# Nystrom attention and two FFN blocks on one core: scores of two batches as 64x32 products, and a written-out order for the rest of the first FFN block

## The chip, the core and the metric

The kernel runs on one NeuronCore of a Trainium2 chip. The metric is the device time of one execution in microseconds (us), lower is better. Five engines work side by side, each through its own instructions in order: TensorE (PE in the profile), VectorE (DVE), ScalarE (ACT), GpSimd (POOL) and SyncE (SP), which issues the DMA transfers here.

## The reference, cut to what matters

```python
def _attn_ref(q, k, v):                  # 4 batches, 8 heads, 576 tokens, 64 dims
    q_lm = q.reshape(B, H, 32, 18, D).mean(axis=3)     # 32 landmarks of 18 tokens
    k_lm = k.reshape(B, H, 32, 18, D).mean(axis=3)
    A, Bm, C = sm(q, k_lm), sm(q_lm, k_lm), sm(q_lm, k)  # softmax(scale * a @ b.T)
    Z = Bm.T / (norm1(Bm) * norminf(Bm) + 1e-06)
    for _ in range(6):
        Z = 2 * Z - Z @ Bm @ Z
    return A @ Z @ C @ v
x = attn_out as (2304 tokens, 512)
h = x @ w_in;   x = (h * clip(h + 3, 0, 6) / 6) @ w_out            # FFN 1, d_ff 2048
h = x @ w_in2;  out = where(h > 0, h, exp(min(h, 0)) - 1) @ w_out2  # FFN 2, d_ff 2048
```

The four weight matrices arrive as float64 and are converted on the chip.

## The kernel before

**Slots of the first FFN block.** FFN 1 is worked through in 128 slots: 4 batches x 2 halves of 288 tokens x 16 blocks of 128 hidden features. (Batch 0 is cut in 320 and 256 tokens.) A slot `i` has two parts. `slot_a1(i)` makes one `h` tile in PSUM by six matmuls (two head groups x three products of high and low parts, `h<-at..,n..`), then ACT takes the Relu (`gf<-h`), DVE multiplies (`gf<-gf,h`), ACT casts the high part (`gh<-gf`) and POOL subtracts for the low part (`gl`). `slot_a2(i - 3)` multiplies the result of three slots ago with `w_out`: four output tiles x three products, twelve matmuls `x<-g..,wo`. The pool for `h` has two PSUM banks, that for `x` four.

**Attention beside the slots.** While the slots of one batch run, the attention of the next is computed in two PSUM banks (`bk`, pool `pa`). Heads come in two groups `g` of four. Per group, `prep` sums tokens to landmarks (`lm`) and POOL lays them out block-diagonally (`bd`, half zeros). `score_b`, `score_c` and `soft` make the three score matrices from `bd` as 128x64 products, two matmuls `pr` beside each other for a half of 288 tokens. `values` transposes the exponentials (`ident,EC`) and multiplies with V (`vt,ect`). `inverse` is the iteration for Z (`BD`, `BT`, `X`), `finish` joins the two (`X,t`). `attn_n` multiplies the outcome (`mt`) with FFN 1's first weights, eight matmuls of 64x32 by 512 columns (`w1c,mt`), and splits them into the `nh`, `nl` that the slots use; `attn_at` does it for A.

**Conversion.** `conv_out2` and `conv_in2` turn 32 pieces of FFN 2's weights from float64 to float32: a load `u` of 512 KB, two ACT steps, two DVE steps, one POOL step (`y`), a store.

**Order.** Up to slot 35 the order of every engine is that of the code (`strict[0]` true: `InOrder` chains each engine's instructions), and the strings `PLAN` and `PLAN1` say in which order the generators take their steps; a letter is one step. From slot 36 (`END`) on `strict[0]` is false: each step is recorded with a due time (`wanted`), and a scheduler orders the engines. `newton(b)` sets the due times of a batch's attention by the slot; `attn_n` and `attn_at` are called at fixed slots (`NAT` = 25, 28, 31 and the batch's first slot); one conversion starts every second slot (`O2`); the loads of FFN 2's input (`load_x(0)`) go one step per slot from slot 100. FFN 2 then runs as 24 `quartet`s of seven products.

Of the kernel before, what the change touches and what calls it, by code (L numbers as in the profile page):

```python
# [10 lines left out]
F32 = mybir.dt.float32  # L11
# [20 lines left out]
def nystrom_ffn_kernel(ctx: ExitStack, tc, q, k, v, w_in1, w_out1, w_in2, w_out2, out):  # L32
# [325 lines left out]
    def conv_out2(kk):  # L358
        to_dram(wo2d[kk], part(w_out2, kk, 0))

    def conv_in2(m, kk):

        to_dram(wi2d[m, kk], w_in2[m, kk], 4)

# [85 lines left out]
    def load_in2(q):  # L450
# [3 lines left out]
        for kk in range(2):  # L454
# [25 lines left out]
            sub(f[:, 0], l[:, 0], f[:, 0])  # L480
            act.copy(out=hr[:, 0:3], in_=l[:, 0:3])
            sub(lr[:, 0:3], l[:, 0:3], h[:, 0:3], pool)
            act.copy(out=hr[:, 3:7], in_=f)
# [7 lines left out]
    kt_t, qt_t, kbd_t, qbd_t, kl_t = {}, {}, {}, {}, {}  # L491

    def load_qk(b, g, what):
        t = ap_.tile([128, 2, S], F32, name=what + "t", tag=what + "t", bufs=2)
        gated(sp.dma_start(out=t, in_=(k if what == "k" else q)[b, g]))
        raw_t[b, g, what] = t
# [128 lines left out]

    def values(b, g, EC, cvs, sc):
# [5 lines left out]
        for j in range(RUN):  # L632
            atr(ct[j // JB][0:PRUN, 128 * (j % JB):128 * (j % JB) + 128], EC[:, j:S:RUN], ident)
        yield 1.0
# [111 lines left out]

    def newton(b):

        EB, sb, sc, cvs = newton_tiles()
        s = [SB * (b - 1) + (NEW if b > 1 else NEW1)]  # L750
        kept = {}

        def go(gen, n=99):
            for _ in range(n):
                wanted(s[0])
                try:
                    s[0] += next(gen) * (PACE if b > 1 else PACE1)
                except StopIteration:
                    return

        def keep(key, gen):
            kept[key] = yield from gen

        go(prep(b, 0))
        go(score_b(b, 0, sb, EB))
        go(keep(0, score_c(b, 0, sc)))
        go(soft(b, 0))
        go(values(b, 0, kept[0], cvs, sc))
        go(prep(b, 1))
        go(score_b(b, 1, sb, EB))  # L770
        inv = keep("Q", inverse(EB, sb))
        sC = keep(1, score_c(b, 1, sc))
        sA = soft(b, 1)
        go(inv, 1)
        go(sC, 2)
        go(inv, 1)
        go(sC)
        go(inv, 2)
        go(sA, 3)
        go(inv, 2)  # L780
        v1 = values(b, 1, kept[1], cvs, sc)
        go(v1, 2)
        go(inv, 2)
        go(sA)
        go(v1)
        go(inv)
        go(finish(b, kept, cvs, sc))

# [498 lines left out]
    def first_half(units, n0):  # L1287
# [38 lines left out]
        for i in range(NKT, END):  # L1326
# [12 lines left out]
    def second_half(slots):  # L1339
# [30 lines left out]
        for e in (act, vec, pool):  # L1370
            e.flow = e.last

# [33 lines left out]
    banks["att"] = ctx.enter_context(tc.tile_pool(name="pa", bufs=2, space=PSUM))  # L1406
    second_half(first_half(units, n0))
    strict[0] = False

    newton(2)  # L1410
    conv = [lambda kk=kk: conv_out2(kk) for kk in range(NKT)]
    conv += [lambda m=m, kk=kk: conv_in2(m, kk) for m in range(NQ) for kk in range(2)]
    for i in range(END, NA):
        b, r = i // SB, i % SB

        wanted(i)
        if r == 0:
            run(attn_n(b, NW - 1))
            run(attn_at(b, 1))
            if b + 1 < B:  # L1420
                newton(b + 1)
# [113 lines left out]
```

## Time and profile before

| | us |
|---|---|
| median of 3 runs | 814.88 (811.93 to 817.96) |
| the profiled execution | 813.47 |
| its span, first to last instruction | 811.7 |

| engine | busy us | share of the span |
|---|---|---|
| PE matmul | 784.1 | 97% |
| PE weight load | 696.9 | 86% |
| DVE | 540.6 | 67% |
| ACT | 461.9 | 57% |
| POOL | 417.3 | 51% |

Durations of matmuls overlap in the profile, since the engine is pipelined: where matmuls follow each other without a wait, the distance from start to start is what one costs. The share of busy time is a mean over stages that have different limits.

### The profile page before, as it was taken

To read this page: it belongs to the slowest core of one execution; us is meant where nothing else is said; L and a number is where in the kernel's file an instruction comes from. 1 tells how busy PE (TensorE), PEld (TensorE's weight loads), DVE (VectorE), ACT (ScalarE), POOL (GpSimd) and SP (SyncE) were. 2 spreads that over 40 slices of the span, in tenths; PEclk is the share of its full clock that TensorE was granted. 3 is DMA by queue.
4 is the path that set the end of the run, shared out by engine and by line. 5 is a ranking of instruction groups with operands and counts; after the bars stand their busy time and mean duration, and the time that the engine had idled before them with its cause. 6 is when DMAs were issued, how large, how long until landed. Compare 5 with 4: busy or idle time off the path is not lost.

```text
span 811.7 us, 16375 instructions
## 1 busy us (share of the span) xinstructions
PE 784.1 (97%) x5928; PEld 696.9 (86%) x5928; DVE 540.6 (67%) x1092; ACT 461.9 (57%) x1012; POOL 417.3 (51%) x423
## 2 busy tenths in 40 slices
PE   7799999999999999989999999999999999999998
PEld 6566678789887889879999998888898989999998
DVE  6899577478645764477345777766655655777795
ACT  3687454666556556584545566556544644555562
POOL 2576476467554565456420786769652550223311
PEclk9899999999999999999999999999999999999999
DMA  9977932786577445752241777689999666877653
GB/s 323 405 221 234 284 118 90 204 267 217 193 231 251 149 144 177 230 192 105 91 173 60 256 262 272 223 309 344 387 381 316 215 223 249 273 237 256 228 183 124
DMA packets 115601, 184.58 MB, mean 227 GB/s; under 512 B 8576, under 2 KB 71552, under 8 KB 115520
## 3 DMA queue, kind: packets, MB, share of 16 engines
q1 hardware_dynamic: 115520, 183.54, 66.5%
q8 instruction: 47, 0.77, 0.4%
q14 instruction: 34, 0.28, 0.1%
HBM read 130.02 MB, written 53.48 MB: 226 GB/s over the span
## 4 chain that ended last, share of the span: by engine, by line
PE 64%; DMA 11%; DVE 9%; ACT 5%; issue 3%; POOL 3%; SPq 1%; DVEq 0%; ACTq 0%; POOLq 0%
PE x L116 33%; PE h L116 27%; PE bk L116 4%; DMA u<-in_moe_w_in 4%; DMA u<-in_moe_w_out 2%; DMA qt<-in_q 2%; DMA w<-wo2d 1%; DVE h L116 1%; DVE u L116 1%; DVE gf L116 1%; ACT gf L116 1%; SPq L116 1%; DVE lm L116 1%; DVE y L116 1%; DMA x<-wo2d 1%
## 5 line engine op out<-in xcount | busy, mean ns | idle before, releaser
L116 PE MATMUL h<-x,wi 128*128 128x384 f32 x1008 | 204.8, 338 | 2.2 <-ACT a L116 1.3
L116 PE MATMUL x<-gh,wo 128*128 128x288 f32 (+1 forms) x896 | 199.3, 297 | 1.0 <-ACT xs L116 0.5
L116 PEld LDWEIGHTS h<-x,wi 128*128 128x128 f32 x1008 | 177.7, 188 | 13.5 <-DVE u L116 2.5
L116 PEld LDWEIGHTS x<-gh,wo 128*128 128x128 f32 x896 | 149.6, 188 | 9.2 <-issue 6.0
L116 PE MATMUL x<-gl,wo 128*128 128x288 f32 (+1 forms) x448 | 130.7, 294 | 0.0
L116 POOL TENSOR_TENSOR gl<-gf,gh 128x288 fp32r<-128x288 f32 (+1 forms) x100 | 85.0, 853 | 76.9 <-ACT gh L116 70.5
L116 ACT CAST gh<-gf 128x288 fp32r<-128x288 f32 (+2 forms) x160 | 72.5, 454 | 88.1 <-DVE gf L116 87.8
L116 PE MATMUL x<-w,gh 128*128 128x512 f32 (+1 forms) x360 | 101.8, 356 | 0.1
L116 PE MATMUL h<-atl,nh 128*128 128x288 f32 (+2 forms) x256 | 82.3, 321 | 7.8 <-DVE gf L116 3.0
L116 DVE SCALAR_TENSOR_TENSOR gf<-gf,y 128x384 f32<-128x384 f32 x80 | 65.6, 820 | 35.6 <-ACT gf L116 35.5
L116 DVE SCALAR_TENSOR_TENSOR gf<-gf,h 128x288 f32<-128x288 f32 (+1 forms) x112 | 49.4, 443 | 55.2 <-ACT gf L116 54.5
L116 PEld LDWEIGHTS x<-gl,wo 128*128 128x128 f32 x448 | 84.3, 188 | 1.1 <-issue 0.9
L116 ACT ACTIVATE gf<-h,half_b 128x288 f32<-128x288 f32 (+2 forms) x128 | 63.5, 499 | 35.9 <-PE h L116 30.9
L116 PE MATMUL x<-w,ghl 128*128 128x512 f32 (+1 forms) x324 | 76.7, 357 | 0.1
L116 PE MATMUL h<-ath,nl 128*128 128x288 f32 (+2 forms) x256 | 76.7, 300 | 0.0
L116 ACT ACTIVATE gf<-y 128x384 f32<-128x384 f32 x80 | 42.0, 525 | 60.4 <-DVE y L116 60.4
L116 PE MATMUL h<-ath,nh 128*128 128x288 f32 (+2 forms) x256 | 76.4, 298 | 0.0
L116 PEld LDWEIGHTS x<-w,gh 128*128 128x128 f32 x360 | 64.7, 189 | 6.4 <-ACT gh L116 0.5
L116 PEld LDWEIGHTS h<-atl,nh 128*128 128x128 f32 x256 | 48.6, 190 | 22.7 <-issue 9.0
L116 PE MATMUL x<-w,gl 128*128 128x512 f32 (+1 forms) x180 | 64.2, 357 | 0.0
L116 POOL TENSOR_TENSOR x<-u,gf 128x384 f32<-128x384 f32 x16 | 18.1, 1156 | 84.8 <-DVE gf L116 50.9
L116 PEld LDWEIGHTS x<-w,ghl 128*128 128x128 f32 x324 | 55.2, 189 | 5.9 <-DVE ghl L116 0.3
(182 smaller groups left out, 1522.6 us busy)
## 6 DMA issues: line engine op xcount, KB each, us to landing
wi<-wi2p SPq DMA_DIRECT2D x64, 448.0 KB, 5.9
wi2p<-wi SPq DMA_DIRECT2D x32, 448.0 KB, 2.8
u<-in_moe_w_in SPq DMA_DIRECT2D x25, 512.0 KB, 5.1
w1c<-w1d SPq DMA_DIRECT2D x48, 256.0 KB, 4.6
w<-wo2p SPq DMA_DIRECT2D x24, 512.0 KB, 6.7
ub<-in_moe_w_out SPq DMA_DIRECT2D x16, 512.0 KB, 10.2
u<-in_moe_w_out SPq DMA_DIRECT2D x16, 512.0 KB, 5.6
wo2p<-w SPq DMA_DIRECT2D x16, 512.0 KB, 3.4
```

What stands on the lines that cost most here:

```text
L116: inst = getattr(self.eng, name)(*a, **kw)
```

## The change

1. For batches 2 and 3 `prep8` sums the landmarks without the division and without `bd`; key landmarks stand in the first 32 columns of the key tile (`n + S` = 608 columns). `products` makes the scores of both groups at once from 64x32 pieces: eight matmuls, four column places x two row halves, each group into a bank of its own. The host lays the heads of odd groups out with row halves swapped, so that the eight pieces lie apart (`a ^ g`).
2. `score_c8` makes the landmark scores and the first half of C in one go (32 + 288 columns); the first half is copied out of PSUM over the keys, so that the second half can have the banks. `soft8` works in the same way by halves.
3. From slot 36 to the end of the first block `strict[0]` stays true. `PLAN2` and `PLAN3` (320 letters each, 160 of them slot steps `s`) write out the order of batches 2 and 3 with the slots (five `s` each) and the conversions (`z`, five each); `ending` does it for slots 100 to 127.
4. `conv_stream` issues each conversion's load one conversion ahead; its `z` steps are used up around slot 90. `load_in2` becomes a generator whose steps are spread from slot 114 on, and `load_x(0)` goes one step per slot from slot 104.

```diff
+    def products(ps, w, x, gs):
+        for pr in range(2):
+            for a in range(2):
+                o = 64 * pr + 32 * a
+                for i, g in reversed(list(enumerate(gs))):
+                    r = slice(64 * (a ^ g), 64 * (a ^ g) + 64)
+                    amm(ps[i][o:o + 32, :], w[i][r, pr, :], x[i][r, pr, :], True, True)
...
+    def score_c8(b, gs, sc, first):
...
+        cut = 0, 32 + HALF, 32 + S
+        ps = []
+        for hf in range(2):
+            ps.append([bank()[:, 0:cut[hf + 1] - cut[hf]] for _ in gs])
+            if hf == 0:
+                first.extend(ps[0])
+            products(ps[hf], ql, [t[:, :, cut[hf]:cut[hf + 1]] for t in kt], gs)
+            yield 0.4
+            if hf == 0 and b:
+                for i in n:
+                    act.copy(out=EC[i][:, 0:HALF], in_=ps[0][i][:, 32:])
...
+        for i, g in enumerate(gs):
+            for hf in (1, 0):
+                act.activation(
+                    out=EC[i][:, hf * HALF:(hf + 1) * HALF], in_=ps[hf][i], func=AF.Exp,
...
+    def soft8(b, gs):
...
+        for hf in range(2):
+            sa.append([bank()[:, 0:HALF] for _ in gs])
+            products(sa[hf], [t[:, :, 0:32] for t in kt], [t[:, :, hf * HALF:(hf + 1) * HALF] for t in qt], gs)
...
+    def conv_stream():
...
+        nxt = begin()
+        while nxt:
+            (gen, o, y), nxt = nxt, begin()
+            flush()
+            yield
+            for _ in gen:
+                yield
+            pending.append((o, y))
+    PLAN2, PLAN3 = "zppspsssppsssspspszspszzzzszssszzcbzz...", "ppszssppzssspzpzsszspsspsszsszszzzcbsz..."
...
-    newton(2)
-    conv = [lambda kk=kk: conv_out2(kk) for kk in range(NKT)]
...
-        if (i - END) % O2 == 0 and conv:
-            gate[0] = marks["slot"]
-            wanted(i + 4)
-            conv.pop(0)()
...
+    zs = conv_stream()
+    for b, plan in ((2, PLAN2), (3, PLAN3)):
+        third(b, plan, slots_of(SB * b - SB + 4, SB * b + 4), zs)
...
+    ending(slots_of(NA - SB + 4, NA), zs, load_x(0, vec), load_in2(0))
```

On TensorE, at the first scores of batch 2 (slot 38 before, slot 39 in the change): `h` and `x` are the slots' matmuls, `bk` the attention banks. Before, the scheduler put the products of one group between two matmuls of a slot; the three other pairs of keys stand apart further down.

```order
L116 MATMUL x<-gh,wo_1311 128x288
L116 MATMUL h<-atl,nh_1950 128x288
L116 MATMUL bk<-lm,bd 64x32 x2
L116 MATMUL bk<-kt,bd 64x288 x2
L116 MATMUL h<-ath,nl_1951 128x288
```

In the change:

```order
L116 MATMUL h<-ath,nl_1951 128x288
L116 MATMUL h<-ath,nh_1950 128x288
L116 MATMUL bk<-kt,lm 32x320 x8
L116 MATMUL x<-gh,wo_1419 128x288
L116 MATMUL x<-gl,wo_1419 128x288
```

Landmark scores and half of C, of both groups, now stand in one piece of eight matmuls behind the six of a slot.

On TensorE, at the start of Z's iteration in batch 2 (slot 47 before, slot 43 in the change); `BD` and `BT` make the norms and the first product. Before, no score product follows within two slots:

```order
L116 MATMUL bk<-BD,onesbd 128x128
L116 MATMUL x<-gh,wo_1873 128x288
L116 MATMUL x<-gl,wo_1873 128x288
L116 MATMUL bk<-BT 32x32 x8
L116 MATMUL x<-gh,wo_1873 128x288
L116 MATMUL h<-atl,nh_1884 128x288
```

In the change:

```order
L116 MATMUL bk<-BD,onesbd 128x128
L116 MATMUL bk<-BT 32x32 x8
L116 MATMUL x<-gh,wo_1652 128x288
L116 MATMUL x<-gl,wo_1652 128x288
L116 MATMUL x<-gh,wo_1652 128x288
L116 MATMUL bk<-qt,kt 32x288 x8
```

Three matmuls of the slot now stand between the products of `BT` and the query scores, which take both attention banks.

On TensorE, in slot 46 of the change: two rounds of the iteration (`X`) and the products with V stand together, where before a round stood alone or behind all 24 products with V.

```order
L116 MATMUL h<-ath,nh_2094 128x288
L116 MATMUL bk<-X 32x64 x8
L116 MATMUL bk<-vt,ect 32x64 x12
L116 MATMUL bk<-X 32x64 x8
L116 MATMUL bk<-vt,ect 32x64 x12
L116 MATMUL x<-gh,wo_1825 128x288
```

In the whole of slots 36 to 127 the attention's matmuls stand in 53 unbroken pieces before and in 34 in the change.

## Rows read from the trace of the kernel before

**Rows 1.** Windows by stage: length, busy us (count) by engine, PE clock, DMA share, GB/s

```profile
161.07:262.03 100.96, 99.49 (x947) 85.61 (x946) 66.15 (x144) 59.69 (x139) 59.75 (x66) 1.00 0.71 232
262.03:357.45 95.42, 93.26 (x898) 82.81 (x896) 55.74 (x126) 58.51 (x134) 54.95 (x58) 1.00 0.57 184
357.45:428.45 71.00, 69.27 (x516) 68.35 (x517) 38.41 (x77) 37.84 (x87) 30.52 (x30) 1.00 0.35 121
```

**Rows 2.** Timeline of PE: start, us, what, xcount; last slot, then the second block

```profile
426.08 0.29 PE L116 MATMUL h<-atl,nh 128*128 128x288 f32 x1
...
428.46 0.34 PE L116 MATMUL h<-x,wi 128*128 128x384 f32 x1
```

**Rows 3.** Waits of PE from 161 us to 428.5 us: total us, times, longest

```profile
PE h L116 <- DVE gf L116: 3.0, 4, 1.3
PE bk L116 <- DVE nl L116: 1.5, 2, 0.8
PE x L116 <- ACT xs L116: 0.5, 1, 0.5
PE bk L116 <- DVE X L116: 0.2, 1, 0.2
```

**Rows 4.** Timeline of PE around one pair of score products

```profile
171.08 0.71 PE L116 MATMUL bk<-kt,bd 128*64 128x288 f32 x4
171.71 0.40 PE L116 MATMUL h<-atl,nh 128*128 128x288 f32 x1
```

**Rows 5.** Timeline of PE around landmark scores alone

```profile
253.82 0.31 PE L116 MATMUL bk<-lm,bd 128*64 128x32 f32 x4
254.06 0.40 PE L116 MATMUL x<-gh,wo 128*128 128x288 f32 x1
```

**Rows 6.** Timeline of PE around eight 64x32 products, 512 columns

```profile
226.25 0.29 PE L116 MATMUL x<-gh,wo 128*128 128x288 f32 x1
226.48 1.09 PE L116 MATMUL bk<-w1c,mt 64*32 64x512 f32 x16
227.50 0.40 PE L116 MATMUL h<-atl,nh 128*128 128x288 f32 x1
227.74 0.29 PE L116 MATMUL h<-ath,nl 128*128 128x288 f32 x1
```

**Rows 7.** Timeline of PE around eight 64x32 products, 256 columns

```profile
162.62 0.66 PE L116 MATMUL bk<-w1c,mt 64*32 64x256 f32 x16
163.21 0.40 PE L116 MATMUL x<-gh,wo 128*128 128x288 f32 x1
```

**Rows 8.** Timeline of PE around one round of the iteration

```profile
207.55 0.43 PE L116 MATMUL bk<-X 32*32 32x64 f32 x16
207.91 0.40 PE L116 MATMUL h<-ath,nh 128*128 128x288 f32 x1
```

**Rows 9.** Waits of PE from 92 us to 161 us (seven rows, five stand)

```profile
PE bk L116 <- POOL bd L116: 1.7, 2, 1.3
...
PE bk L116 <- DVE nl L116: 0.4, 1, 0.4
PE bk L116 <- ACT EC L116: 0.4, 1, 0.4
PE bk L116 <- DVE X L116: 0.3, 1, 0.3
PE bk L116 <- DVE nn L116: 0.2, 1, 0.2
```

**Rows 10.** Timeline of DVE, start of the iteration in batch 1

```profile
126.28 0.28 DVE L116 TENSOR_REDUCE nn<-bk 128x4 f32<-128x128 f32 x1
...
127.27 0.41 DVE L116 SCALAR_TENSOR_TENSOR X<-bk,cc,istack 128x32 f32<-128x32 f32 x2
```

**Rows 11.** Waits of ACT from 161 us to 357 us, the two for conversion loads

```profile
ACT y L116 <- DMA u<-in_moe_w_out: 14.8, 9, 3.4
ACT y L116 <- DMA u<-in_moe_w_in: 12.3, 7, 3.1
```

**Rows 12.** DMA issues from 161 us to 357 us: count, KB, median us to landing

```profile
u<-in_moe_w_in SPq DMA_DIRECT2D x16, 512.0 KB, 4.9
```

More of the change, by code (lines that the diff above doesn't have):

```diff
@@ L356, in split_out1 @@
         wo[kk] = h, l
[L358 to L363, printed above, removed]
     def scratch(n, w):
@@ L631, in values @@
         ct = [bank(), bank()]
-        for j in range(RUN):
+        for j in [*range(JB, RUN), *range(JB)] if b > 1 else range(RUN):
             atr(ct[j // JB][0:PRUN, 128 * (j % JB):128 * (j % JB) + 128], EC[:, j:S:RUN], ident)
+        if 1 < b < B - 1:
+            load_qk(b + 1, g, "k")
         yield 1.0
@@ L745, in newton_tiles @@
         return EB, sb, sc, cvs
[L747 to L787, printed above, removed]
     PLAN = """
@@ L1325, in first_half, with slots_of @@
         run(ns)
-        for i in range(NKT, END):
+        yield from slots_of(NKT, END)
+    def slots_of(n0, n1):
+        for i in range(n0, n1):
             wanted(i)
@@ new lines, in third, with keep, preps, parts @@
+    def third(b, plan, slots, zs):
+        EB, sb, sc, cvs = newton_tiles()
+        kept, first, gs = {}, [], range(G)
+        def keep(key, gen):
+            kept[key] = yield from gen
+        def preps():
+            for g in gs:
+                yield from prep8(b, g)
+        def parts():
+            for c in range(NW):
+                yield from attn_n(b, c)
+        make = {
+            "p": preps, "c": lambda: keep("C", score_c8(b, gs, sc, first)), "b": lambda: score_b8(gs, first, sb, EB),
+            "i": lambda: keep("Q", inverse(EB, sb)), "a": lambda: soft8(b, gs),
+            "v": lambda: values(b, 0, kept["C"][0], cvs, sc), "V": lambda: values(b, 1, kept["C"][1], cvs, sc),
+            "f": lambda: finish(b, kept, cvs, sc), "n": parts, "t": lambda: attn_at(b, 0), "T": lambda: attn_at(b, 1),
+        }
+        gens = {"s": slots, "z": zs}
+        for c in plan:
+            if c not in gens:
+                gens[c] = make[c]()
+            next(gens[c], None)
+        run(slots)
+        for c in "pcbiavVftnT":
+            run(gens[c] if c in gens else make[c]())
@@ L1375, in nystrom_ffn_kernel, with ending @@
+    def ending(slots, zs, xs, ws):
+        for i in range(NA - SB + 4, NA):
+            for n in range(NDM + 1):
+                next(slots, None)
+                if i < NA - SB + XSET + 4:
+                    next(zs, None)
+                elif n == 2:
+                    next(xs, None)
+                if i >= NA - 14 and n == 4:
+                    next(ws, None)
+        run(slots)
+        run(zs)
+        run(xs)
+        run(ws)
     win, xp = [], []
```

149 lines of the change are left out of this document (111 added, 38 removed).

## Prediction

> **What bounds the kernel now.** I read the windows by stage first, cut where slots begin: the change touches slots 36 to 127, which run from 161.07 to 428.45 us. PE is busy for 262.0 of these 267.4 us, DVE for 160, ACT for 156, POOL for 145; the granted clock is 1.00 in all three stages, full speed [rows 1]. So PE is the bound, and the other engines matter only where PE waits for them. The timeline of PE gives the price of a slot without attention: 426.08 to 428.46, 2.38 us for 18 matmuls, 0.132 us each [rows 2]. The 92 slots cost 92 x 2.38 = 219.0 us by that; the other 48.4 us are attention on PE and waits. The list of PE's waits says how much is waiting: 3.0 + 1.5 + 0.5 + 0.2 = 5.2 us idle [rows 3]. Some 43 us are attention matmuls with what they cost at their edges. That is what the change can win from: 5 us of waits, and the attention's own 43.
>
> The second block does not enter the sum. Both programs have the same PE order there, and I leave its time as it is.
>
> **Price of an attention piece.** A piece costs more than from its first start to the next slot matmul. Around the piece at 226.48 the matmul ahead lasts 0.23 instead of 0.13, and the one behind it, from 227.50 to 227.74, 0.24: 0.09 + 0.10 = 0.19 us for entry and exit [rows 6]. With this each piece's price is (next slot matmul - start) + 0.19:
>
> - one pair of score products, 288 columns: 171.71 - 171.08 + 0.19 = 0.82 us [rows 4];
> - a landmark score pair alone: 0.24 + 0.19 = 0.43 [rows 5];
> - eight 64x32 products: 1.02 + 0.19 = 1.21 at 512 columns [rows 6], 0.59 + 0.19 = 0.78 at 256 [rows 7]; so 0.0017 us a column, 0.83 at 288 and 0.89 at 320;
> - one round of the iteration alone: 0.36 + 0.19 = 0.55 [rows 8].
>
> **Term 1, the scores.** Before, batches 2 and 3 have 16 pairs and four landmark pairs. 16 x 0.82 = 13.1, and the landmark pairs add at least their bare 0.24 each, 14.1 together; some share an edge with another piece, some stand alone. I take 14.1. After, each batch has one group at 320 columns and three at 288: 0.89 + 3 x 0.83 = 3.4, 6.8 for both. The groups have the form of the `w1c,mt` pieces, eight 64x32 pieces over the whole array, so the price is that of a row. **-7.3 us.** The trace has no group in which one row half writes both banks; see the third rival.
>
> **Term 2, fewer edges.** 53 pieces become 34. Of the 19, seven are score pieces, already counted (15 that held scores alone against 8), and one is a 256-column piece that merely moves ahead of slot 36. That leaves eleven merges. At 0.19 each they would give 2.1; but four only join transposes of the same kind, whose edges are thin, and V's products are cut in two. Between 0 and 2.1 I take 6 x 0.19 = **-1.1 us**.
>
> **Term 3, the waits of today: -5.2 us** [rows 3]. 1.5 of it is `attn_n`: the batch's third and fourth call stand a slot apart, and the fourth finds its banks not yet emptied by DVE (`nl`). In the change five slots lie between them in batch 2 and seven slot steps in batch 3. 3.0 is an `h` product that finds DVE late with `gf`.
>
> **Term 4, new waits.** A plan fixes where PE asks for a bank, and PE then holds everything behind it, the slots too. The nearest evidence is the written-out order of batch 1, from 92 to 161 us. There PE waited 4.0 us for others, 1.7 of it for `bd`, which batches 2 and 3 no longer have [rows 9]. What is new is that each score group takes both attention banks, so it waits until both former users are read out. Batch by batch:
>
> - Query scores behind `BT` (slots 43 and 75). The second bank is free when DVE has gone from `nn` to the second `X`: 126.28 to 127.27 + 0.41, 1.40 us [rows 10]. On PE only three slot matmuls stand in between, 0.40 plus an edge. About **1.0 us** of wait; in batch 1 it was 0.2, as only the first bank was wanted there [rows 9].
> - `BD` behind the exponentials of C: two banks again, and three of four exponentials must be through. In batch 1 one such wait was 0.4 [rows 9]; I take **0.4**.
> - Two dense pieces, where a round of the iteration follows the last with twelve small products between (slots 46 and 50): **0.3** each, as `DVE X` in batch 1 [rows 9].
> - One late `nl` at **0.4** [rows 9].
>
> That is 2.4 a batch, 4.8 for both. Of the 3.0 us for `gf` I keep 1.0: DVE's steps of `load_x` are still there, but one per slot. The plan spreads the rest. **+5.8 us.** Bounds: 2.0 if only the wait behind `BT` is real; 15.5 if all 267.4 us go at batch 1's rate of 4.0 in 69 us.
>
> What I cost at nothing: the landmark sums keep their count on DVE; POOL loses the `bd` products; ACT gains two copies a batch. All of it lies under PE, with ACT and POOL 58 to 61% busy in the first two stages [rows 1]. Where they come too late, it is in term 4. Keys of batch 3 are loaded later than before (behind V's transposes), but that is still some 18 slots ahead of their use.
>
> **Sum.** 813.47 (the profiled execution: 811.7 span and 1.8 around it) - 7.3 - 1.1 - 5.2 + 5.8 = 805.7 us; I say **805.5**. That is 1.2% under the shown median of 814.88, and 1.0% under the profiled execution itself.
>
> The Trainium skill, page "TensorEngine Tiling (Array Packing)", section "PSUM Bottleneck", warns that packing the array does not speed up emptying PSUM, which may become the limit. By that the whole gain of term 1 could turn into bank waits, and the time would be about 813. The rows agree in kind, since batch 1's waits are nearly all for ACT or DVE reading a bank.
>
> **Rivals.**
>
> *Waits hardly matter (797 to 802).* Only the wait behind `BT` is left: 813.47 - 7.3 - 1.1 - 5.2 + 2.0 = 801.9; with full edges and no waits 798.9. For it: the scheduler's order before had 0.2 us of `X` waits in two batches [rows 3]. Against it: there no group took two banks. Chance 0.20.
>
> *Bank hand-over eats the gain (810 to 816).* PE idles at batch 1's rate: + 15.5 instead of 5.8, 815.2. For it: same style of order, same two banks, and both are now asked for together. Against it: batch 1 has 16 slots for what here has 32. Chance 0.17.
>
> *The row halves don't overlap (809.5).* Within a group, each row half writes both banks, at different partitions. If that kept the halves apart, a group would stream its columns twice: 8 x 288 x 0.0017 = 4.0 us more, 809.5. Against it: a round of the iteration has eight 32x32 pieces in four row places, all writing one bank. With no overlap it would stream 512 columns, 1.0 us like [rows 6]; it took 0.36 [rows 8]. Chance 0.05. The same page of the Trainium skill, section "Gotcha 1: PSUM Pressure", says that different row tiles cannot access one PSUM bank at the same time; by that it would be this 809.5, and [rows 8] does not agree with it.
>
> *Slower (above 823): ACT held by conversion loads.* The 32 conversions are drawn together, from slots 36 to 98 into 36 to 90, and ACT's order is now fixed. From the plan's letters a load is issued 1.0 to 3.6 slots before ACT wants it; eight of the 32 have less than 1.5 slots, some 4 us, and the median landing is 4.9 [rows 12]. Today ACT waits 16 times, 27.1 us in total [rows 11], and 3.0 us reach PE as late `gf` [rows 3]: two banks for `h` absorb the rest. It decides from 18 us on PE: 805.5 + 18 = 823.5, that is 0.55 us from each of 32 loads. Since today's 27 us of ACT waits give 3, it would take six times as much to get through. Chance 0.08.
>
> **How the numbers follow.** The forecast (802 to 810) has 0.50. A measurement of this kernel can tell about 1% from no change, so faster means under 806.7 us and slower over 823.0. Faster: the first rival's 0.20 and 0.32 of the forecast's 0.50, since 805.5 stands close to the line: 0.52. Same: the other 0.18, 0.17 and 0.05: 0.40. Slower: 0.08. The range is 797 to 815: its low end is no waits and all edges less the spread of runs, its high end batch 1's rate of waits.
>
> **What the profile would show.** Term 1: pieces `bk<-kt,lm` and `bk<-qt,kt` of 16 records, 0.64 to 0.70 us from start to the next slot matmul; about 1.15 would be the third rival. Term 3: no wait of PE for `nl` over 0.5 us. Term 4: in the list of PE's waits from slot 36 to the second block, `DVE X` or `nn` about 1 us in each batch, in all 4 to 8 us; over 12 would be the second rival. The slower case would show `PE h` waiting for `gf` by more than 10 us, with ACT behind `u`. The prediction is wrong in its ground if the second block, which I held fixed, moves by more than 2 us.

## The result

The change takes 818.28 us (median of 20 runs, 812.95 to 823.32); the kernel before, run beside it, 814.05 (20 runs). The ratio is 1.0053, interval [1.0029, 1.0078]: half a per cent slower where 805.5 us and a gain of 1% were forecast, and above the range of 797 to 815. The profiled execution took 821.63 us. Where its time lies, beside the profile of before:

| part | before, us | change, us | difference |
|---|---|---|---|
| start to slot 36 | 161.07 | 166.51 | +5.4 |
| slots 36 to 67 | 100.96 | 100.66 | -0.3 |
| slots 68 to 99 | 95.42 | 96.79 | +1.4 |
| slot 100 to the second block | 71.00 | 70.17 | -0.8 |
| second block, to the span's end | 383.2 | 385.7 | +2.5 |
| around the span | 1.8 | 1.8 | 0 |

The windows of the change, cut at the same places (columns as in [rows 1]):

```profile
0.00:166.51 166.51, 151.99 (x1464) 115.92 (x1465) 116.43 (x271) 97.33 (x225) 90.89 (x110) 0.93 0.68 226
166.51:267.17 100.66, 94.05 (x945) 83.81 (x943) 63.76 (x142) 62.40 (x143) 59.84 (x59) 1.00 0.72 234
267.17:363.96 96.79, 93.84 (x951) 83.96 (x943) 58.01 (x135) 56.60 (x132) 53.75 (x55) 1.00 0.54 169
363.96:434.13 70.17, 67.42 (x507) 66.73 (x506) 34.24 (x75) 37.79 (x86) 27.43 (x29) 1.00 0.36 122
434.13:819.85 385.72, 377.37 (x2126) 349.60 (x2124) 267.86 (x471) 209.35 (x433) 180.70 (x156) 1.00 0.73 255
```

In slots 36 to 67 PE was busy 99.49 of 100.96 us before [rows 1] and is busy 94.05 of 100.66 now. So PE's work did shrink by 5.4 us there, and the stage is 0.3 us shorter: the gain became idle time. What PE waits for between slot 36 and the second block (total, times, longest), to be read against [rows 3]:

```profile
PE h L116 <- DVE gf L116: 8.5, 8, 2.2
PE bk L116 <- ACT kt L116: 2.1, 4, 1.0
PE bk L116 <- DVE mt L116: 1.1, 1, 1.1
PE x L116 <- ACT xs L116: 0.5, 1, 0.5
```

12.1 us in all where it was 5.2. The wait for `nl` is gone as forecast; the one for `gf` has nearly trebled. The longest of these waits shows how. ACT stands still for 7 us at the first of its steps in a conversion:

```profile
201.85 0.49 ACT L116 ACTIVATE gf<-h,half_b 128x288 f32<-128x288 f32 x1
209.31 0.66 ACT L116 ACTIVATE y<-u 128x512 f32<-128x512 f32 x1 [6.97 <-DMA wo2d<-y]
209.87 0.66 ACT L116 ACTIVATE u<-u 128x512 uint32<-128x512 uint32 x1
210.43 0.41 ACT L116 CAST gh<-gf 128x288 fp32r<-128x288 f32 x1
```

Behind the waiting step stand the `gh` and `gf` steps of the slots, so the slots' chain stops too, and PE with it:

```profile
209.29 0.29 PE L116 MATMUL x<-gh,wo 128*128 128x288 f32 x1
211.79 0.40 PE L116 MATMUL h<-atl,nh 128*128 128x288 f32 x1 [2.21 <-DVE gf L116]
```

The step waits because `y` has two buffers and the store of the one it wants has not landed. That store was issued at 201.92 us behind three loads for batch 3 of 576 KB each, with a fourth right after it (SyncE's queue: start, duration of the issue, what):

```profile
197.19 2.08 SPq L116 DMA_DIRECT2D qt<-in_q  x2
199.48 0.56 SPq L116 DMA_DIRECT2D kt<-in_k  x1
200.15 0.53 SPq L116 DMA_DIRECT2D u<-in_moe_w_out  x1
201.92 0.33 SPq L116 DMA_DIRECT2D wo2d<-y  x1
203.11 0.33 SPq L116 DMA_DIRECT2D vt<-in_v  x1
```

It landed 7.3 us later; in quieter stretches of this trace such a store took 2 to 3 (the one at 193.47 us took 2.2). ACT's waits in conversions from slot 36 to 99, to be read against [rows 11]:

```profile
ACT y L116 <- DMA wo2d<-y: 13.3, 6, 7.0
ACT y L116 <- DMA wi2d<-y: 8.7, 5, 3.7
...
ACT y L116 <- DMA u<-in_moe_w_out: 3.6, 1, 3.6
```

The sum is the same as before (25.6 against 27.1 us). The last column is not: 7.0, 3.7 and 3.6 where it was 3.4 and 3.1. And eleven of the twelve waits are now for a buffer to be stored, where all sixteen were for loads.

The score groups themselves cost what was forecast. One of them, on PE:

```profile
194.28 0.29 PE L116 MATMUL h<-ath,nh 128*128 128x288 f32 x1
194.50 0.72 PE L116 MATMUL bk<-qt,kt 64*32 64x288 f32 x16
195.15 0.40 PE L116 MATMUL x<-gh,wo 128*128 128x288 f32 x1
```

Eight products (sixteen records) in 195.15 - 194.50 + 0.19 = 0.84 us, for a forecast of 0.83. Four of the eight groups cost more, 1.08 to 1.39; i1 below shows why.

### The profile page after: what moved, and what is told of

It reads as the page before. It is cut to its first block, busy times and chain, and to the rows that moved or that the text cites. A ratio compares the mean times of both kernels' runs of the same rounds, so it can differ in the third digit from the quotient of the medians.

```text
span 819.8 us, 16460 instructions
## 1 busy us (share of the span) xinstructions
PE 784.7 (96%) x5976; PEld 700.0 (85%) x5976; DVE 540.3 (66%) x1092; ACT 463.5 (57%) x1016; POOL 412.6 (50%) x407
## 5 line engine op out<-in xcount | busy, mean ns | idle before, releaser
L116 PE MATMUL x<-gh,wo 128*128 128x288 f32 (+1 forms) x896 | 203.6, 298 | 0.5 <-ACT xs L116 0.5
L116 PEld LDWEIGHTS h<-x,wi 128*128 128x128 f32 x1008 | 177.5, 188 | 14.8 <-DVE u L116 4.0
L116 DVE SCALAR_TENSOR_TENSOR gf<-gf,y 128x384 f32<-128x384 f32 x80 | 70.0, 875 | 35.7 <-ACT gf L116 35.7
```

The source lines that it names most:

```text
L116: inst = getattr(self.eng, name)(*a, **kw)
```

## Experiments

Each kernel was timed beside the kernel before on the same chip and has one profile. "Stretch" is slot 36 to the start of the second block; waits are PE's in it; ACT is the longest wait of ACT within a conversion. For the kernel before the stretch is 267.4 and 266.0 us in two profiles.

| run | ratio [95%] | stretch | PE waits, of them gf | ACT longest | second block |
|---|---|---|---|---|---|
| change | 1.0053 [1.0029, 1.0078] | 267.6 | 12.1, 8.5 | 7.0 | 385.7 |
| e0_again | 1.0043 [1.0016, 1.0070] | 268.8 | 12.1, 9.9 | 7.7 | 387.2 |
| e1_lead2 | 1.0269 [1.0228, 1.0311] | 292.9 | 26.9, 13.9 | 7.6 | 386.5 |
| e2_even | 1.0173 [1.0135, 1.0212] | 278.4 | 18.7, 7.7 | 6.0 | 388.3 |
| e3_scores | 1.0068 [1.0039, 1.0097] | 269.3 | 7.7, 2.4 | 3.7 | 385.7 |
| b0_before | 1.0004 [0.9973, 1.0036] | 266.0 | 4.0, 2.5 | 3.0 | 384.4 |
| f1_loads | 1.0003 [0.9978, 1.0028] | 266.9 | 11.3, 6.3 | 3.7 | 387.3 |
| f2_sums | 1.0047 [1.0021, 1.0073] | 269.5 | 14.7, 8.2 | 7.1 | 386.5 |
| f3_tail | 1.0051 [1.0024, 1.0079] | 270.5 | 12.9, 10.1 | 8.4 | 387.3 |
| g1_pad | 1.0012 [0.9985, 1.0040] | 265.8 | 10.9, 6.5 | 6.8 | 386.3 |
| g3_beforepad | 1.0034 [1.0007, 1.0061] | 268.0 | 5.9, 2.3 | 4.0 | 386.1 |
| g2_all | 1.0115 [1.0079, 1.0150] | 272.3 | 13.6, 9.9 | 6.3 | 386.7 |
| i1_split | 1.0078 [1.0050, 1.0106] | 271.8 | 10.4, 8.1 | 7.5 | 385.3 |
| i2_loadspad | 1.0030 [0.9998, 1.0062] | 265.8 | 8.9, 4.8 | 4.0 | 385.1 |
| i3_beforepad2 | 1.0133 [1.0089, 1.0178] | 268.6 | 6.1, 2.9 | 3.7 | 384.3 |
| h1_half | 1.0048 [1.0020, 1.0076] | 271.3 | 12.2, 4.0 | 5.2 | 385.6 |
| h2_more | 1.0057 [1.0035, 1.0080] | 265.7 | 10.2, 4.7 | 4.5 | 388.6 |

The stretch holds one cost that the other columns do not show: TensorE's granted clock. Over the stretch it is 1.00 in both profiles of before and in the change, f1, f2, g1, g3, h2 and i3, 0.99 in e0, e3, f3, g2, i1 and i2, 0.98 in e2 and h1 and 0.97 in e1. The lower level comes with a wait of PE. In e0, slot 48 (PE's timeline, then a window with columns as in [rows 1]):

```profile
208.51 0.40 PE L116 MATMUL h<-atl,nh 128*128 128x288 f32 x1 [3.20 <-DVE gf L116]
```

```profile
209.60:213.00 3.40, 3.40 (x17) 3.37 (x16) 2.19 (x6) 2.64 (x6) 2.23 (x3) 0.50 0.28 92
```

Half the clock for 3.4 us costs some 1.7 us (an estimate from this row), over half as much again as the wait itself. All 18 such falls in the stretches of these runs stand at a wait of PE or within 1.5 us of its end. Not every wait brings one: the one of 2.21 us in the first profile of the change did not. So the stretches of e1, e2, g2 and h1, with two to six falls each, are longer by more than the waits in the table.

### Is it the start, the conversions or the scores?

**e0_again**: the change unaltered.

> The change once more, unaltered. The trace of the change lost 5.4 us against that of before ahead of slot 36 (slot 36 starts at 166.51 us instead of 161.07), where TensorE's instructions are the same, with the granted clock at 0.66 and 0.83 of full speed in the windows 20 to 40 us and 40 to 60 us (before: 0.83 and 1.00). Theory 'start': that part is the luck of one execution; here slot 36 starts anywhere from 160 to 168 us, and the stretch from slot 36 to the second block stays at 267 to 268.5 us. Theory 'layout': the change itself makes the start slower; slot 36 starts at 166 us or later again.

Slot 36 starts at 161.66 us here (166.51 in the first profile, 162.27 in a second profile of before). The 5.4 us at the start belong to that execution: its mean granted clock up to slot 36 is 0.93, against 0.97 here, with the same instructions. The waits of the stretch come back at the same places: ACT 7.7 us, then PE 3.2. The stretch is 0.3 us above the range given for it; the fall of the clock shown above is in it.

**e1_lead2**: conversion loads issued two ahead instead of one.

```diff
-        nxt = begin()
-        while nxt:
-            (gen, o, y), nxt = nxt, begin()
+        ahead = [begin() for _ in range(2)]
+        while ahead[0]:
+            ahead.append(begin())
+            gen, o, made = ahead.pop(0)
```

> Each conversion's load is issued two conversions ahead instead of one, nothing else is altered. In the trace of the change TensorE waits 8.5 us for gf between slot 36 and the second block, 5.7 us of it up to slot 100, and ScalarE waits 22.0 us for what the conversions load or store. Theory 'conversions' (ScalarE, in its fixed order, stands behind a conversion's data): waits of ScalarE for conversions under 12 us, TensorE's wait for gf up to slot 100 under 3 us, the stretch from slot 36 to the second block 262 to 265 us instead of 267.6. Theory 'banks' (the score groups' hand-over of both banks takes the gain): stretch 267 to 268.

Far slower: PE waits 14.8 us longer than in the change, and the six falls of the clock make up most of the rest. ACT's waits grow to 44 us; as I read it, since a longer lead keeps more loads in the same queue ahead of the stores (the run also takes the tile `y` later, at ACT's first step):

```profile
ACT y L116 <- DMA wi2d<-y: 18.7, 8, 4.5
ACT y L116 <- DMA wo2d<-y: 13.3, 8, 3.8
ACT y L116 <- DMA u<-in_moe_w_out: 12.3, 2, 7.6
```

Issuing the loads earlier did not free ACT; this form of the theory fell, and the stretch lies far outside the rival's range too.

**e2_even**: the 192 conversion steps spread evenly, one after every second step of a slot.

```diff
-        third(b, plan, slots_of(...), zs)
+        third(b, even(plan), slots_of(...), zs)   # one z after every second s
```

> The conversions' steps are taken out of the two plans and put back evenly, one after every second slot step, so that 32 conversions spread over slots 36 to 100 as before and no longer meet in the dense slots; all other letters keep their order. Theory 'conversions': the longest wait of ScalarE for a conversion falls from 7.0 us to under 4, the stretch is 262 to 265 us. Theory 'banks': the stretch stays at 267 us or grows, as the attention's steps stand where they stood.

ACT's waits fall to 10 us, yet PE waits longer: one of ACT's, for a load, is 6.0 us (4.5 on PE), and the queue now makes PE wait for the next weights:

```profile
PE h L116 <- DVE gf L116: 7.7, 6, 4.5
PE bk L116 <- DMA w1c<-w1d: 4.3, 1, 4.3
```

The sum of ACT's waits does not tell what PE pays.

**e3_scores**: the kernel before with the 64x32 scores alone, in the scheduler's order.

```diff
-        for g in gs: ... score_c(b, g, sc) ... soft(b, g)
+        sC = keep("C", score_c8(b, gs, sc, first)); sA = soft8(b, gs)
```

> The kernel before with one part of the change alone: the 64x32 score products of both groups at once (with the copies and layouts they need), ordered by the scheduler; no written-out order from slot 36, conversions every second slot. Theory 'conversions': the scores' gain of 7 us on TensorE shows, the stretch from slot 36 to the second block is 259 to 262 us instead of 267.4, the median 806 to 808. Theory 'banks': TensorE's waits on bk grow from 1.7 us to 6 or more, the stretch is 265 us or longer.

Few waits (7.7 us) and still no gain, even without the one fall of the clock in its 269.3 us. The scheduler split seven of the eight groups: it issued the first product when its bank came free and slot matmuls while the other bank was not. PE's timeline:

```profile
174.34 0.67 PE L116 MATMUL bk<-kt,lm 64*32 64x288 f32 x2
174.94 0.40 PE L116 MATMUL x<-gl,wo 128*128 128x288 f32 x1
...
175.40 0.71 PE L116 MATMUL bk<-kt,lm 64*32 64x288 f32 x14
176.04 0.40 PE L116 MATMUL x<-gh,wo 128*128 128x288 f32 x1
```

One product costs 174.94 - 174.34 + 0.19 = 0.79 us and the other seven 0.83: each part streams 288 columns. Without the idle time recorded in them, all attention pieces cost 40.2 us here, against 41.8 before and 34.1 in the change.

**i1_split** tests that reading: the change with the first product of each group one step ahead. (The expectation counts sixteen products; they are eight, with two records each.)

```diff
                     amm(ps[i][o:o + 32, :], w[i][r, pr, :], x[i][r, pr, :], True, True)
+                    if first:
+                        first = False
+                        yield 0          # and "csc", "asa" for "c", "a" in the plans
```

> The change, with the first of the sixteen products of each of the eight score groups issued one step of a slot ahead of the other fifteen, as the scheduler left seven of the eight in the run of the scores alone. Theory 'a group costs one stream of its columns however many products are in it': the lone first product costs 0.8 us, the rest 0.83 to 0.89 as before, so the eight groups cost 6.4 us more and the stretch from slot 36 to the second block goes from 267 to 273 or 274; ratio 1.010 to 1.014. Rival 'only the edge is paid twice': 8 x 0.19 = 1.5 us more, the lone product about 0.3 us, stretch 268 to 269; then the run of the scores alone lost its gain elsewhere.

```profile
186.82 0.67 PE L116 MATMUL bk<-qt,kt 64*32 64x288 f32 x2
187.42 0.40 PE L116 MATMUL x<-gh,wo 128*128 128x288 f32 x1
...
188.01 0.71 PE L116 MATMUL bk<-qt,kt 64*32 64x288 f32 x14
188.65 0.40 PE L116 MATMUL x<-gh,wo 128*128 128x288 f32 x1
```

Six lone products cost 0.79 to 0.86 us; two that stand with a round of the iteration 0.7. The pieces together cost 39.1 us (34.1), 5.0 more, and the stretch is 4.2 longer than in the change's first profile and 3.0 longer than in e0, which has one fall of the clock as i1 has. Stretch (271.8) and ratio lie between the ranges of the two theories; the prices of the pieces decide. The stream theory holds; the edge alone would have been 1.5. It came out under 6.4 because four of the whole groups had paid for late banks (1.08, 1.21, 1.21 and 1.39 us, recorded idle time apart), and the split covers that.

### Which waits are the 8.5 us for gf?

In the first profile they stand at three places: behind conversions (slots 39, 40 and 48: 3.1 us), behind batch 3's landmark sums (slots 69 and 70: 2.6) and behind the second block's first loads (slots 117 to 121: 2.7). In the kernel before all four stand from the end of slot 99 on, among the second block's first tokens and weights. The list of PE's waits from 161 to 357.4 us has none for `gf`; from 357.4 to 428.5 us it has

```profile
PE h L116 <- DVE gf L116: 3.0, 4, 1.3
```

and ACT had begun its last conversion before that:

```profile
354.10 0.67 ACT L116 ACTIVATE y<-u 128x512 f32<-128x512 f32 x1 [0.44 <-DMA u<-in_moe_w_in]
```

So the 27.1 us for which ACT waited in conversions before [rows 11] cost PE no wait for `gf` at all; in the change 25.6 us cost 3.1.

**f1_loads**: batch 3's four query and key loads one at a time.

```diff
-                load_qk(b + 1, g, "q")
+                later.append(lambda g=g: load_qk(b + 1, g, "q"))
+            if c == "s" and k >= 70 and k % 10 == 0 and later:
+                later.pop(0)()
```

> The change, with the four query and key loads of batch 3 (576 KB each) issued one at a time at slots 50, 52, 54 and 56 instead of three of them within 2.3 us at slot 45 and one at slot 51. Theory: ACT's wait of 7.0 us at 202 to 209 us (the conversion that waits for the store of its buffer, 6.9 us in flight beside those loads) goes below 2, PE's wait of 2.2 us for gf there goes, and the stretch from slot 36 to the second block falls from 267.6 by 2 to 3 us. Rival 'the conversions hold ACT there whatever else is loaded' (a conversion's store and the next load queue behind one another): ACT still waits 5 us or more in slots 44 to 50, and the stretch stays within 1 us.

```profile
ACT y L116 <- DMA wo2d<-y: 8.6, 5, 3.2
ACT y L116 <- DMA wi2d<-y: 8.5, 6, 3.7
ACT y L116 <- DMA u<-in_moe_w_out: 3.7, 1, 3.7
```

The 7 us wait is gone, and with it PE's 2.2 at slot 48: that link is shown. A gain in time is not. The ratio is that of before, but the stretch is only 0.7 us shorter than in the change's first profile (the 1.9 against its second are mostly that profile's fall of the clock), which is inside the rival's "within 1 us", and g1 below, with no edit to the order, has a shorter one still. The second block is no shorter either. The mean clock of f1's runs was 0.9904 against e0's 0.9888, and by the line at the end of this document that makes 1.1 us of the 3 us between their ratios. No run gave `y` a third buffer, which would test the store alone.

**f2_sums**: the eight sums taken ahead to slots 60 to 67.

```diff
-    PLAN3 = "ppszssppzssspzpzsszspsspss..."
+    PLAN2 = "...sssqss..." (slots 60 to 67);  PLAN3 = "szsszssss..."
```

> The change, with the eight landmark sums of batch 3 on DVE (0.74 us each) taken from slots 68 to 70, where they stand between the subtractions that make gf, to slots 60 to 67, one a slot. Theory 'queue order': the waits of PE for gf at 271.9 and 275.8 us (1.3 us each) go and nothing takes their place; the stretch falls by 2 to 2.6 us. Rival 'DVE is short of time': DVE's other work in slots 60 to 67 (nl, 0.65 us each) is then late, with waits for nl or gf there, and the stretch stays within 1 us.

```profile
PE h L116 <- DVE gf L116: 8.2, 7, 2.2
PE bk L116 <- ACT kt L116: 4.1, 5, 2.1
```

One of the two `gf` waits went. In its place a conversion's store met the eight loads of `w1c` at 268 to 274 us: ACT waited 5.2 us, and PE 2.1 for `kt`. Nothing gained.

**f3_tail**: slots 100 to 127 with the old loop and the scheduler.

```diff
-    ending(slots_of(NA - SB + 4, NA), zs, load_x(0, vec), load_in2(0))
+    strict[0] = False
+    for i in range(NA - SB + XSET, NA): ...   # the loop of before
```

> The change up to slot 99; from slot 100 to the end of the first block the old loop and the scheduler's order (the second block's token and weight loads by priority). Theory 'queue order': the three waits of PE for gf at 406 to 418 us (2.7 us) go, as the kernel before has only 0.2 us of them after slot 108, and slots 100 to the second block fall from 70.2 us to 68 or less. But the kernel before took 71.0 there: rival 'the scheduler is no better', 70 to 71 us again, with waits elsewhere. The second block's tokens come at other places in the queues: if its 2 to 4 us more over the kernel before come from this, it falls back to 383; otherwise it stays at 385 to 387.

71.4 us from slot 100 (70.2 with the written order, 71.0 before): there are `gf` waits again, 0.7 to 1.0 us at slots 102, 103 and 105, where the kernel before has its own. The order of the end cost nothing, and the second block did not come back.

**g2_all**: f1 and f2, eight conversion steps moved from slots 38 and 69 to 71 into later ones, one slot more between the second block's first weight loads and their use, and the padding of g1 below.

```diff
+            yield                        # load_in2, behind the loads
-    ... 38: zspszzzzszss   69: spzpzsszsps
+    ... 38: zspszsss       69: szssss         # z put into slots 47, 56, 79, 81, 84, 86
```

> The change with all that seems to cost it time mended together: batch 3's loads spread over slots 50 to 56, its landmark sums over slots 60 to 67, four conversion steps of slots 38 and four of 69 to 71 put into later slots, one slot more between the load of the second block's first weights and their use, and the padding of PE's instruction stream. Theory: of the 8 to 10 us that PE waits for gf, 2 to 4 are left, the stretch from slot 36 to the second block falls from 267.6 to 261 to 264, the second block to 384; ratio 0.993 to 0.997, faster than both kernels. Rival 'a fixed order only moves the waits' (as the landmark sums did alone): waits for gf go and waits for kt, mt or xs come, the stretch stays at 266 or more, and the ratio is 1.000 or above.

```profile
PE h L116 <- DVE gf L116: 9.9, 8, 2.8
```

The rival was right: the steps that were moved met other stores, with waits of ACT of 5.0 and 6.3 us where the change has 2.7 and 3.7 within a slot. Behind each of them PE waited (2.8 and 2.6 us) and the clock fell.

**h1_half** and **h2_more**: f1 with five, or six, of the sums taken ahead, conversions left where they are; h2 also with the extra slot at the end.

> The change with batch 3's loads spread over slots 50 to 56 and five of its eight landmark sums taken ahead, one each in slots 62, 63, 65, 66 and 67, the other three one a slot from 68; conversions as in the change. Theory 'cover': a wait of ACT up to about 3 us costs PE nothing, so with the longest one cut by the loads and DVE's run of sums broken up, the gf waits at the start of batch 3 (2 x 1.3 us) go as well; stretch 263 to 265, ratio 0.995 to 0.999 if no new wait of ACT is over 3.5 us. Rival 'a fixed order moves the waits': a new one over 4 us appears, stretch 266 or more, ratio 1.000 or above.

> As the run before it, with six sums ahead (slots 60 to 67) and two in slots 68 and 69, and one more slot between the load of the second block's first weights and their use. Theory 'cover': beside the gf waits at batch 3's start, 1 to 2 us of the 2.3 at 403 to 414 us go; stretch 262 to 264, ratio 0.993 to 0.998. Rival: the waits at the end move into the second block's first tokens, as they did in the run with all edits (0.85 and 0.90 us there); ratio 1.000 or above.

h1 got a wait of ACT of 5.2 us at batch 3's start and 2.5 us of PE for `kt` with it, and three falls of the clock, which make its stretch 271.3 with no more waiting than the change. h2 had the same wait of ACT a little shorter (4.5 us), with 1.7 us of PE for `kt`:

```profile
PE bk L116 <- ACT kt L116: 3.9, 5, 1.7
```

Its stretch is 265.7 us, not the 262 to 264 expected, with two waits that g2 had too (0.9 us each) at the second block's first tokens, as the rival said. No version that I ran beats the kernel before.

### Why is the second block longer?

It has PE's instructions in the same order in every kernel, and took 383.2 and 384.4 us in two profiles of before, 385.1 to 388.6 in fourteen of changed kernels.

**b0_before**: the kernel before, unaltered.

> The kernel before, unaltered, for a second profile of it. Two things in its first profile may be of that one execution only: slot 36 starts at 161.1 us (166.5 and 161.7 in two profiles of the change), and the second block lasts 383.2 us (385.7 and 387.2 in the change). Theory 'the second block is slower in the change': here the second block lasts 382.5 to 383.9 again. Rival 'spread between executions': it lasts 385 or more. For the start: between 161 and 167 by either, since both programs have the same instructions ahead of slot 36. Ratio 1.000 within 0.3%.

384.4 lies between the two theories. The clock fell to its lower level once in this second block, which it did not in the first profile (granted 0.51 in this window):

```profile
526.80:530.20 3.40, 3.40 (x11) 2.92 (x10) 1.88 (x4) 2.98 (x8) 3.40 (x3) 0.51 0.68 270
```

That fall is in the 384.4, so the difference to the changed kernels stands.

Where it arises can be read matmul by matmul, since the order is the same. Against the first profile of before, the change is 0.5 us late at 119 us into the block and 2.1 us late at 141, and stays so to its last matmul. From 141 us on no profile gains or loses more than 0.2 us. At 119 us the other profiles are 0.4 to 3.0 us behind that first one of before, b0 among them (2.9, with its fall of the clock): the wait of 0.8 us for `gl` that the change has at 18 us is in b0 too.

What recurs is one wait of PE for `u`, some 123 us into the block: 1.1 to 2.4 us in every changed kernel without padding, absent before. ACT there waits for a load `w<-wo2d`, queued behind four loads of `wi`. The first of these lands after 4.4 and 3.9 us in the two profiles of before, 6.3 in both of the change. The DMA view of the same 7.7 us, in the change (540.4 to 548.1 us) and then in before (534.8 to 542.5); a queue's row gives packets, MB and share, the row of an issue count, KB each and median us to landing:

```profile
q8 instruction: 1, 0.02, 1.0%
q14 instruction: 1, 0.01, 0.7%
wi<-wi2p SPq DMA_DIRECT2D x4, 448.0 KB, 7.0
```

```profile
wi<-wi2p SPq DMA_DIRECT2D x4, 448.0 KB, 5.4
```

In the change an instruction fetch of 16 KB lies among the loads (one packet, 1.3 us on its DMA engine, 110.6 us into the block) and one of 8 KB of another queue; before, the 16 KB ones lie at 91 and 117 us.

**g1_pad**, **g3_beforepad**, **i3_beforepad2**, **i2_loadspad**: small matmuls in PE's warm-up, 33 in the change, 15 and 33 in the kernel before, 33 in f1.

```diff
+                for _ in range(11):      # three times; 5 in g3
+                    pe.matmul(warm[0:32, 0:1], lhsT=ident[0:32, 0:32], rhs=ident[0:32, 0:1], ...)
```

> The change with 33 small matmuls (32x32 by one column) added to PE's warm-up in the first slots, results unused. They move nothing behind them but PE's place in its instruction stream, by about 130 records, half of the some 256 that one 16 KB fetch of instructions brings. In all six profiles of changed kernels one such fetch (0.9 to 1.3 us on a DMA engine) falls 110.4 to 112.4 us into the second block, on the four loads of wi there, the first of which lands after 5.9 to 6.8 us; in the two profiles of the kernel before the fetches fall at 91 and 117 us and the same load lands after 3.9 to 4.4. Theory 'instruction fetch': here the fetches fall near 97 and 124 us, the load lands in 4.0 to 4.8 us, PE's wait for DVE u of 1.2 to 2.4 us at 123 to 126 us goes, and the second block falls from 385.7 to 387.3 to 383 to 385; the ratio falls by 0.002 to 0.003 against the change. Rival 'another cause' (where the tiles lie): the load still takes 6 us and the second block stays at 386 to 387.

> The kernel before with 15 such small matmuls in the warm-up, about 60 records, which should bring its fetch of instructions from 117 us into the second block to some 110 or 111, where it lies in the changed kernels. Theory 'instruction fetch': the first load of wi there goes from 3.9 to 4.4 us to about 6, PE waits 1 us or more for DVE u at about 123 us, and the second block goes from 383.2 and 384.4 to about 386; ratio 1.002 to 1.004. Rival 'another cause': all stays, ratio 1.000.

> The kernel before with the same 33 small matmuls in the warm-up as in the padded change. If the fetches of instructions decide the second block's time, they fall near 103 and 130 us there, clear of the loads of wi at 106 to 113, the first of these lands in 4 to 4.5 us and the second block lasts 383 to 384.5. If any move of PE's stream against the other queues costs it (as with 15 of them, where no fetch of PE's lay on the loads and the second block still took 386.1), it lasts 385.5 or more again, and the kernel before as it stands is the lucky one of the family.

> The change with the two edits that each brought it back towards the kernel before: batch 3's loads spread over slots 50 to 56, and the 33 small matmuls in the warm-up. Theory: the two add up, stretch 265 to 266.5, second block 385.5 to 386.5, ratio 0.996 to 0.999. Rival: what they brought is within what any edit does to the order of loads; ratio 1.000 to 1.003. If it is under 0.997 with its interval under 1, it beats both kernels.

| profile | 16 KB fetch, us into the block | first wi lands after | PE's wait for u |
|---|---|---|---|
| before, b0 | 91 and 117 | 4.4, 3.9 | 0 |
| i3 (33 in before) | 105 and 133 | 4.6 | 0.3 |
| g2, g1, i2 (33 in changed kernels) | 95 to 97 and 119 to 122 | 4.8, 5.3, 5.3 | 0.2, 0.7, 0.7 |
| g3 (15 in before) | 85 and 115 | 5.3 | 1.2 |
| change, e0, e1, e2, e3, f1, f2, f3, h1, h2, i1 | 110 to 114 | 5.7 to 7.0 | 1.1 to 2.4 |

Padding PE's stream moved these fetches, so they are PE's own. With no 16 KB fetch on the loads the first of them lands within 5.3 us in seven profiles of seven, and with one after 5.7 or more in eleven of eleven. With few exceptions, the longer it takes, the longer PE waits. For i3 (0.3 us of this at the place in question, 0.6 later):

```profile
PE h L116 <- DVE u L116: 0.8, 2, 0.6
```

So the fetch costs this wait about 1 us: 1.76 falls to 0.70 from the change to g1, 1.57 to 0.70 from f1 to i2. It is not all. g1's block still takes 386.3, since it is 2.2 us late at 119 us, ahead of this wait. And g3 did not test what it was built for: its fetch came at 115 us and not at 110 or 111, so that no fetch lay on the loads; the forecast of 386 for its block came true by another way. What makes the block's first 119 us differ by up to 3 us from profile to profile stays open. The Trainium skill, page "Runtime: NRT & Kernel Launch", section "Instruction fetch mechanics", says that instructions come in blocks of 16 KiB through a queue of the engine's own, and that the cost is mostly hidden. The trace agrees on the block (one packet of 16 KB); the loads beside it are not spared, and PE pays the 1 us above for them.

In the ratios the padding pays for what it gains. The mean clock over the timed runs of the three kernels with 33 products is 0.9845 to 0.9863, against 0.9888 for e0 and 0.9904 for f1. So i2 has the stretch that was expected of it (265.8) and a shorter second block, and its ratio still misses the range given, with 1.0030. In i3 the products, at 37 to 50 us, stand mostly at the lower level, and slot 36 starts at 170.25 us:

```profile
0.00:170.25 170.25, 154.55 (x1514) 119.19 (x1515) 120.81 (x279) 96.99 (x223) 92.33 (x116) 0.92 0.67 221
40.20:53.80 13.60, 12.83 (x107) 10.73 (x108) 7.62 (x16) 6.44 (x14) 6.46 (x5) 0.50 0.50 170
```

In g1, with the same products, it starts at 164.15: how much of this the products cost and how much differs by execution is not settled.

## Why the prediction was wrong

**Terms 1 and 2, price of the scores and edges: right.** Forecast -8.4 us together; all attention pieces without idle time in them cost 41.8 us before and 34.1 and 34.3 in two profiles of the change, -7.6. (The edge is 0.10 + 0.11 = 0.21 us by its own rows, not 0.19; that moves the two terms by some 0.3.) The rival that row halves do not overlap fell: 0.84 us a group, not 1.3. By the Trainium skill, page "TensorEngine Tiling (Array Packing)", section "Gotcha 1: PSUM Pressure", the halves could not use one bank at the same time; the groups, at 0.84 us, do not agree.

**Term 3, today's waits: the `nl` part right, the `gf` part wrong** (below). The 0.5 us for `xs`, put down as gone, stayed.

**Term 4, new waits: right in size.** Forecast 4.8 us. Measured 2.1 for `kt` (ACT's copies and exponentials of C, which hold both banks; 1.5 of it at `BD` and `BT` of batch 2), 1.1 for `mt` (an input of the products that wait), and 1.5 inside the four dearer groups: 4.7. That the sum fits is in part luck. The places were not those of the forecast: behind `BT`, put at 1.0 a batch, it was 0.25 and 0.55.

**The step that failed is "of the 3.0 us for `gf` I keep 1.0", with what was put at nothing beside it.** Measured were 8.5 us, in three parts. At the end of the first block, where all of the 3.0 had stood, 2.7 stayed. The landmark sums, under "what I cost at nothing", gave 2.6, since they stand between the `gf` steps in DVE's fixed order. The conversions gave 3.1. For these the sum has no term, and the slower rival's argument that kept them out is a misreading: it says that 27 us of ACT's waits give 3 on PE, so that six times as much would be wanted. But the 27.1 us end at 354 us, and the 3.0 us for `gf` begin at the wait that ends at 357.45, behind DVE's steps of `load_x`, as Term 4 itself has it. The 27 us had cost PE no wait for `gf`. A rate of 3 in 27 would even fit the change's 3.1 for 25.6, by luck. What decides is the length of the single wait: it is covered up to a length that its place in the order sets, and PE pays the rest. Two places at which several kernels have a long wait show it:

| place | ACT waits, us | PE then waits for gf, us | difference |
|---|---|---|---|
| slot 39 | 3.59, 3.61, 3.70, 3.83, 4.14, 4.26, 4.72 | 0.61, 0.63, 0.72, 0.85, 1.16, 1.28, 1.74 | 2.98 each |
| slot 48 | 6.78, 6.97, 7.11, 7.50, 7.61, 7.71, 8.43 | 1.85, 2.21, 2.17, 2.58, 3.11, 3.20, 3.71 | 4.5 to 4.9 |

(From the change, e0, e1, f1, f2, f3, g1, i1 and h2; one more, of 4.06 at slot 39 in i1, gave 0.40. Waits of 2.37 and 2.67 there, in g1 and i2, gave none.) Elsewhere the cover was 1.5 (e2, slot 38) to 3.8 (g2, slot 80), and at slots 73 and 79 waits of up to 5.2 reached no `gf` at all. Before, the longest wait is 3.4 us, and [rows 11] say so in their last column: sixteen waits, each inside the cover of its place. The change has the same sum in fewer and longer ones. My rival named loads. That holds for the wait at slot 39; the long one at slot 48 is for a store, issued among batch 3's loads, and f1, which moved these loads, took it away. Of the sums, f2 shows one of the two waits (1.3 us); that the 2.7 us are the second block's loads is read from the trace, and f3, which took the written order away there, got as much in other slots.

**The second block held fixed: wrong.** +2.5 us in the profile, and +1.3 to +4.8 in the fourteen profiles against the mean of the two of before; more, in nine of them, than the 2 us at which I had called the prediction wrong in its ground. The instruction fetch accounts for about 1 us of it; the rest is open.

**The sum after the fact.** 813.47 + 5.4 (the clock at the start) + 0.2 (stretch: 7.6 less in the pieces, 6.9 more of waits, and 0.9 that I did not trace) + 2.5 = 821.6, the profiled execution. Without the start and the second block that is 813.7. The second rival's 815.2 is near it by luck: banks and `mt` took 4.7 us of waiting, the slots' own chain 8.5.

## What to carry to other kernels

Price a queue that other work crosses by its longest waits against the cover of the consumer's buffers, not by their sum: 27 us of ACT's waits cost PE no wait for `gf` in pieces of up to 3.4 us, and 25.6 us cost 3.1 when single waits reached 3.6 and 7.0. And look where both stand in time before one is divided by the other. A product that packs many small pieces has to be issued whole, since each part pays the full stream of columns; a scheduler that fills bank waits will split it, and an order that keeps it whole pays those waits as idle time. A long wait of PE can cost more than itself, through the clock. And a few tiny products that nobody uses can cost 0.3%, so half a per cent is shown only beside such a control.

## What was not expected of the hardware

- Fifteen 32x32 products of one column in the warm-up of the kernel before, with nothing else changed, gave a ratio of 1.0034 [1.0007, 1.0061] (g3).
- A 16 KB instruction fetch occupies one DMA engine for 0.9 to 2.1 us. The first load of `wi` beside it landed after 5.7 to 7.0 us, without one after 3.9 to 5.3.
- The granted clock explains much of the spread. Over 123 timed runs of before, a straight line gives 0.67 us less for each 0.001 more of mean clock (residual 1.7 us). Brought to 0.990 by it, e0's twelve runs mean 818.9 us against 817.7 for before: some 1.1 of its 2.6 us are the kernel's own, and the rest is a mean clock of 0.9888 against 0.9911. Even the 1.1 is not clear of chance: b0's ten runs, the kernel before itself, come to 818.7 by the same line. Whether the clock is lower because of the change is not settled. Most of the lower level lies ahead of slot 36, where both kernels have the same instructions; but the one fall in e0's stretch, behind PE's wait of 3.2 us, takes 0.002 off that execution's mean, about as much as the whole difference.
